# New orders for two convolutions and two attention layers, a softmax normalized on TensorE, and row statistics read from PSUM

## The chip, the cores and the metric

The kernel runs on one core of a Trainium2 chip. A core has several engines with instruction queues of their own: TensorE (PE in the profile, with its weight loads as PEld), VectorE (DVE), ScalarE (ACT), GpSimd (POOL) and SyncE (SP), which here only issues transfers. Each engine takes its instructions strictly in the order in which they were issued to it; an instruction that needs another engine's result waits at the head of its queue, and everything behind it waits too. SBUF is the working memory, PSUM the small memory into which TensorE writes its sums. The metric is the device time of one execution in microseconds (us).

## The reference, cut to what matters

The input u has 2048 tokens of 512 features. Two kinds of layers alternate, A, B, A, B, with the same weights in both rounds, and each adds its result to x:

```python
x = A_u
x = x + A(layernorm(x));  x = x + B(layernorm(x))
x = x + A(layernorm(x));  x = x + B(layernorm(x))

# A: a convolution along the tokens, done by FFT
P = exp(dt * A[:, :, None] * l);  K = einsum("dn,dnl,dn->dl", C, P, dt * B).real
y = irfft(rfft(u, 4096) * rfft(K, 4096))[:2048] + u * Dskip

# B: attention of 32 heads (16 features each) over 8 keys, 2 tokens apart, behind each token
q, k, v = split(x @ wqkv)
logits = einsum("bhsd,bhswd->bhsw", q, kg) * 16 ** -0.5      # kg, vg: k, v at s, s-2, ..., s-14
o = einsum("bhsw,bhswd->bhsd", softmax(logits), vg) @ wo
```

The spectrum of K depends on the weights alone, so it is computed once and used by both A layers.

## The kernel before, in words

The work falls into five stretches that follow one another.

**Spectrum of K.** `kgen` builds tables of powers, multiplies them, turns the sums into the spectrum, stores it in DRAM (`kt_scratch`), and normalizes x and does the first half of the forward transform of the first A layer beside it, into the tile `Z`. It runs by a written order: the string `KGEN`, whose words each name a step. Words that begin with `@` are steps of the first convolution.

**A convolution** (`a_steps`) goes over 16 groups of 32 features, numbered 0 to 15. A group passes through a pipeline of one-letter steps on four engines:

- `T`: TensorE transposes 8 blocks of `Z` into PSUM (tile `pt`, line 246);
- `t` or `a`: VectorE (`t`) or ScalarE (`a`) copies them to SBUF (`zt`, line 252);
- `X`: TensorE, second half of the transform (`xp`, line 258; its PSUM pool `psX` holds one tile, so `X` of a group waits until the tile of the group in front has been copied out);
- `c`: ScalarE copies `xp` to `xc` (line 264);
- `p`: VectorE multiplies by the spectrum `Kt` (`pab`, line 271); then `k` loads a later group's `Kt` on SP;
- `v`: TensorE, inverse transform (`vp`, line 287); `V`: ScalarE copies it to the tile `VT` (line 291). Group 15 is done in two halves; the second ones are `i` and `I`.

The first convolution's order is the end of `KGEN`; the second's is made from the same words. After the last `p`, VectorE computes four rows of one lane each for the lag 2048 (`kU`, lines 311 and 313), which only the last quarter of y needs.

**y and its norm.** `y_rows` (lines 323 to 327) makes two rows of tokens in one PSUM tile `ps_y` (pool `psS`, two tiles): two matmuls with `VT`, sometimes one for lag 2048, and one that adds x. A row needs all 512 features, so all 16 groups of `VT`; the first tile alone does columns 0 to 479 of its two rows first, which need groups 0 to 14 only. ScalarE copies the tile to x (line 1454); VectorE computes the rows' statistics from the copy (line 1117), and the rows are normalized (lines 1123 to 1133), transposed (1147) and copied (1150).

**Attention** (`b_layer`). TensorE projects q and k (1164) and v (1251); VectorE multiplies q by k shifted by each of the 8 offsets (`prodqk`, 1212 and 1214), TensorE sums over a head's features (`Lp`, 1236); the softmax follows; v, shifted by transfers (1275), is multiplied by the weights on VectorE (`prodpv`, 1346), summed by TensorE (`po`, 1356), copied by ScalarE (`oT`, 1367) and multiplied by wo (1385, plus x, 1390). Heads go in four groups i, tokens in two halves jh. The softmax of (i, jh): maximum over the keys (VectorE and TensorE, 1295 to 1303); for i = 2, 3 TensorE subtracts it with the matrices `ident` and `nident` in PSUM and ScalarE takes exp from there (1313 to 1316); TensorE sums over the keys (1321); ScalarE takes Ln and then Exp of the negative (1323, 1324); VectorE multiplies by that (1325). In the first B layer the rows of x are then normalized again and put through the first half of the next transform (`N`, lines 1430 and 1433).

**The order.** The instructions of y, its norm and the attention are planned in `b_layer` as small operations with names (`y0a`, `n0b`, `L103a`, `S20g`, `P38k`; the last letter counts the operations of a block). The long strings in `LAYERS` give the order in which they are issued, one string for each round; a `+` behind a name chooses VectorE (or the second of two engines) for an operation that can run on either. `Plan` estimates times only to decide how many dummy columns TensorE streams into a gap (line 1079); it moves nothing.

Of the kernel before, what the change touches and what calls it, by code (L numbers as in the profile page):

```python
# [11 lines left out]
ACT = mybir.ActivationFunctionType  # L12
# [95 lines left out]
def make_small_consts(nc, const):  # L108
# [11 lines left out]
    small = [("order", _bf(order), BF), ("ident", _bf(np.eye(128)), BF), ("nident", _bf(-np.eye(128)), BF),  # L120
# [10 lines left out]
    nc.gpsimd.memset(C["zero"][:], 0.0)  # L131
    C["eps"] = const.tile([128, 1], F32, name="eps")
# [76 lines left out]
def a_steps(nc, tc, C, Ng, kt_dram, load_w, layer, Z, es, es_y, psS=None):  # L209
# [44 lines left out]
    def second_stage(cg):  # L254
        xps[cg] = psX.tile([128, 2, 512], F32, name="xp", tag="psX")
# [4 lines left out]
    def second_stage_out(cg):  # L260
        xc, xp = fwork.tile([128, 8, 1, 128], BF, name="xc", tag="xc"), xps.pop(cg)
        xcs[cg] = xc
        for gs in parts(cg):
            nc.scalar.copy(xc[:, gs].rearrange("q g o l -> q (g o l)"), xp[:].rearrange("q h n -> q (h n)")[:, gs.start * 128:gs.stop * 128])  # L264

    def times_spectrum(cg):
        pab, xc, kt = pabp.tile([128, 8, 2, 128], BF, name="pab", tag="pab"), xcs.pop(cg), kts.pop(cg)
        pabs[cg] = pab
        for gs in parts(cg):
            n = gs.stop - gs.start  # L270
            a.last = nc.vector.tensor_tensor(pab[:, gs], xc[:, gs].to_broadcast([128, n, 2, 128]), kt[:, gs], ALU.mult)  # L271
        if layer and cg + KT_BUFS[layer] < 16:
            load_k(cg + KT_BUFS[layer])
        if cg == 14 and layer == 0:
            load_w()
# [13 lines left out]
    def inverse_out(cg, part=0):  # L289
        dst = VT[:].rearrange("k r j d -> k (r j) d")[:, :, cg * 32:(cg + 1) * 32].rearrange("k q (e g) -> k q e g", e=GE)  # L290
        nc.scalar.copy(dst[..., parts(cg)[part]], vps.pop((cg, part))[:].rearrange("k g (q e) -> k q e g", e=GE))  # L291

    a.step = dict(T=transposes, t=transposed, a=lambda cg: transposed(cg, True), X=second_stage, c=second_stage_out,
                  p=times_spectrum, v=inverse, V=inverse_out, i=lambda cg: inverse(cg, 1), I=lambda cg: inverse_out(cg, 1), k=load_k)
# [3 lines left out]
def a_layer(nc, tc, C, Xg, Ng, kt_dram, layer, Z, es_z, a=None):  # L298

    if a is None:  # L300
        with ExitStack() as es:
            es.enter_context(es_z)
            a = a_steps(nc, tc, C, Ng, kt_dram, None, layer, Z, es, ExitStack())
            with tc.manual_schedule():
                for word in KGEN.split():
                    if word[0] == "@" and word[1] != "k":
                        a.step[word[1]](int(word[2:]))
    VT, F1T, psS, tag, ident = a.VT, a.F1T, a.psS, "psg" if layer == 0 else "psS", C["ident"]
    kU = Ng[NG - 1]
    with tc.issue_after(a.last.ins):  # L310
        nc.vector.tensor_tensor(kU[0:1], Ng[0][0:1], C["klast"][:].unsqueeze(1).to_broadcast([1, 4, D]), ALU.mult)
# [1315 lines left out]
```

## Time and profile before

| | us |
|---|---|
| median of 3 runs (lowest, highest) | 425.97 (425.73, 428.2) |
| the profiled execution | 425.74 |
| its span, first to last instruction | 424.0 |
| VectorE busy | 398.6 |
| TensorE matmuls busy | 374.4 |
| ScalarE busy | 332.2 |

A profile shows one execution. "Busy" is the time in which an engine works on at least one instruction; two instructions of one engine may overlap a little, so the mean time of an instruction is longer than the distance from its start to the next one's start. In a row of a timeline the first number is the start, the second the time that the row covers, "x4" the instructions merged in it, and the bracket the idle time ahead of it with what ended it. The granted clock of TensorE is 1.00 throughout.

### The profile page before, as it was taken

The numbers are of one execution on the slowest core, as the hardware profiler recorded it, in microseconds if no ns is written. First come the engines' busy times: TensorE is split into PE (matmuls) and PEld (weight loads), VectorE is DVE, ScalarE is ACT, GpSimd is POOL, SyncE is SP. The second block draws the span as 40 slices with busy tenths as digits, with TensorE's granted clock in tenths as the row PEclk, the third lists the DMA queues.
The fourth block names the chain that finished last, engine by engine and source line by source line (L and its number), as shares of the span: only waits on it lengthen the run. The fifth ranks groups of instructions, "written<-read, shape, count | busy, mean of one in ns | idle before, by whom it ended". The sixth has DMA issues, their size and how long they took to land.

```text
span 424.0 us, 12183 instructions
## 1 busy us (share of the span) xinstructions
PE 374.4 (88%) x5072; PEld 258.1 (61%) x5112; DVE 398.6 (94%) x732; ACT 332.2 (78%) x602; POOL 25.5 (6%) x66
## 2 busy tenths in 40 slices
PE   1167998999989999999997899789999999996996
PEld 1033685676468755686865565278845686875563
DVE  5999999999889989899999999979989999999994
ACT  6999999998989989767655499989988676663542
POOL 5000011011210000002010000000000001200000
PEclk9999999999999999999999999999999999999999
DMA  7900002253889940005281061249300009350022
GB/s 227 430 32 0 2 17 52 74 162 109 254 242 280 300 146 3 2 2 119 58 175 52 2 198 54 100 117 284 101 0 4 2 2 162 69 123 2 22 80 101
DMA packets 25790, 44.06 MB, mean 104 GB/s; under 512 B 7301, under 2 KB 17222, under 8 KB 25094
## 3 DMA queue, kind: packets, MB, share of 16 engines
q1 hardware_dynamic: 22918, 38.09, 30.7%
q0 software_dynamic: 1856, 4.53, 4.8%
q8 instruction: 40, 0.66, 0.7%
q10 hardware_dynamic: 960, 0.66, 0.5%
q14 instruction: 16, 0.13, 0.1%
HBM read 29.01 MB, written 6.95 MB: 85 GB/s over the span
## 4 chain that ended last, share of the span: by engine, by line
PE 36%; DVE 28%; ACT 13%; issue 9%; DMA 3%; SPq 1%; DVEq 0%; ACTq 0%
DVE prodpv L1346 11%; PE ps_qk L1164 8%; DVE prodqk L1214 5%; PE ps_v L1251 4%; PE psg L578 3%; PE Lp L1236 3%; ACT Z L1433 2%; DVE Z L481 2%; PE psk L545 2%; DVE zt L252 2%; ACT xc L264 2%; DMA V<-V 2%; PE ps_y L327 2%; PE ps_y L323 2%; PE pt_x L1147 2%
## 5 line engine op out<-in xcount | busy, mean ns | idle before, releaser
L1346 DVE TENSOR_TENSOR prodpv<-V,Lsb 128x2048 bf16<-128x2048 bf16 x64 | 75.4, 1220 | 0.1
L1164 PE MATMUL ps_qk<-xnT,wqk 128*128 128x512 bf16 x256 | 60.1, 379 | 0.0
L1212 DVE TENSOR_TENSOR prodqk<-qT,N 128x1024 bf16<-128x1024 bf16 (+3 forms) x88 | 42.5, 541 | 2.1 <-ACT N L1167 1.8
L1214 DVE TENSOR_TENSOR prodqk<-qT,N 128x1024 bf16<-128x1024 bf16 (+3 forms) x56 | 40.6, 764 | 0.2 <-ACT qT L1167 0.2
L1356 PEld LDWEIGHTS <-prodpv 128*128 128x128 bf16 x1024 | 34.3, 98 | 9.6 <-DVE prodpv L1346 3.8
L271 DVE TENSOR_TENSOR pab<-xc,Kt 128x2048 bf16<-128x2048 bf16 (+1 forms) x34 | 39.1, 1159 | 0.9 <-ACT xc L264 0.6
L1356 PE MATMUL po<-halves,prodpv 128*128 128x64 bf16 x1024 | 37.3, 193 | 2.6 <-DVE prodpv L1346 2.6
L1164 PEld LDWEIGHTS <-wqk 128*128 128x128 bf16 x256 | 23.7, 98 | 23.5 <-DVE xnT L1150 0.2
L264 ACT CAST xc<-xp 128x1024 bf16<-128x1024 f32 (+1 forms) x34 | 35.7, 1066 | 1.4 <-PE pt L246 0.7
L291 ACT CAST VT<-vp 128x1024 bf16<-128x1024 f32 (+1 forms) x34 | 35.6, 1098 | 0.0
L287 PEld LDWEIGHTS <-pab 128*128 128x128 bf16 x512 | 30.9, 98 | 6.8
L287 PE MATMUL vp<-sb_IC,pab 128*128 128x128 bf16 x512 | 33.3, 219 | 0.6
L1385 PE MATMUL ps_o<-wo_t,oT 128*128 128x512 bf16 x122 | 31.9, 379 | 0.6
L1236 PEld LDWEIGHTS <-prodqk 128*128 128x128 bf16 x1024 | 29.4, 96 | 4.8 <-DVE prodqk L1214 1.9
L1367 ACT CAST oT<-po 128x512 bf16<-128x512 f32 x32 | 17.7, 587 | 18.4 <-PE po L1356 18.4
L1236 PE MATMUL Lp<-sb_bones,prodqk 128*128 128x8 bf16 x1024 | 30.3, 166 | 1.4 <-DVE prodqk L1214 1.2
L1251 PE MATMUL ps_v<-wv,xnT 128*128 128x256 bf16 x256 | 30.3, 272 | 0.0
L505 PE MATMUL psadd<-Z,sb_ident 128*128 128x512 bf16 (+3 forms) x72 | 18.7, 342 | 12.8 <-DVE Z L481 6.9
L1258 ACT CAST V<-ps_v 128x512 bf16<-128x512 f32 x32 | 18.6, 586 | 13.2 <-PE ps_v L1251 13.0
L1117 DVE BATCH_NORM_STATS2 ln_stats<-X 128x6 f32<-128x512 bf16 x39 | 24.9, 680 | 2.4 <-ACT X L1454 2.4
L1167 ACT CAST N<-ps_qk 128x512 bf16<-128x512 f32 x32 | 18.5, 590 | 10.4 <-PE ps_qk L1164 10.1
L1251 PEld LDWEIGHTS <-xnT 128*128 128x128 bf16 x256 | 24.3, 98 | 3.6
(195 smaller groups left out, 820.0 us busy)
## 6 DMA issues: line engine op xcount, KB each, us to landing
Kt<-kt_scratch SPq DMA_DIRECT2D x60, 256.0 KB
kt_scratch<-ks SPq DMA_DIRECT2D x32, 128.0 KB
G<-c_G SPq DMA_DIRECT2D x2, 1536.0 KB
V<-V SPq DMA_DIRECT2D x8, 288.0 KB
X<-in_A_u_dram SPq DMA_DIRECT2D x4, 512.0 KB
F1Tsb<-c_F1T SPq DMA_DIRECT2D x2, 1024.0 KB
V<-V SPq DMA_DIRECT2D x4, 512.0 KB
V<-V POOLq DMA_DIRECT2D x4, 384.0 KB, 8.4
```

The lines of the kernel that those rows point to most:

```text
L264: nc.scalar.copy(xc[:, gs].rearrange("q g o l -> q (g o l)"), xp[:].rearrange("q h n -> q (h n)")[:, gs.start * 128:gs.stop * 128])
L271: a.last = nc.vector.tensor_tensor(pab[:, gs], xc[:, gs].to_broadcast([128, n, 2, 128]), kt[:, gs], ALU.mult)
L287: a.last_pe = nc.tensor.matmul(vp[:, g, :], pabs[cg][:, gs.start + g, ab, :], C["IC"][:, ab, :], start=(ab == 0), stop=(ab == 1))
L291: nc.scalar.copy(dst[..., parts(cg)[part]], vps.pop((cg, part))[:].rearrange("k g (q e) -> k q e g", e=GE))
L1164: nc.tensor.matmul(t.ps[:], wqk[:, ct, f0:f0 + 128], x_group(g)[:, :, ct], start=(ct == 0), stop=(ct == 3))
L1212: nc.vector.tensor_tensor(b.pr[:, u:u + 2 * n, 1 - halves_of[0], :], q, cols(kT[i][:, starts[0]:starts[0] + n * 128]), ALU.mult)
L1214: nc.vector.tensor_tensor(b.pr[:, u:u + 2 * n].rearrange("f u a q -> f a u q")[:, ::-1], q.unsqueeze(1).to_broadcast([128, 2, 2 * n, 64]), ...
L1236: nc.tensor.matmul(t.Lp[:, w, u % 2, u // 2, :], b.pr[:, u].rearrange("f a q -> f (a q)"), bones[:], start=False, stop=(t.parts == W // 2 ...
L1251: nc.tensor.matmul(t.ps[:, jj, :], tokens(ct, jp * 2 + jj, c), wv[:, ct, fp * 256:(fp + 1) * 256], start=(jj + ct == 0), stop=(jj == 1 and ...
L1346: nc.vector.tensor_tensor(t.p2[:, c:c + k, 0:nj, :].rearrange("p c j (d h) -> p c j d h", d=DH), m.V2[i // 2][:, c0 + c:c0 + c + k, r0:r0 ...
L1356: nc.tensor.matmul(po[jj // k][:, jj % k, c, :], t.p2[:, c - c0, jj, :], fold, start=(first and c == c0 and jj % k == 0), stop=(last and c ...
L1385: nc.tensor.matmul(t["ps"][:], m.oT[:, ft, j * 128:(j + 1) * 128], wo_t[:, ft, :], start=(start and ft == lo), stop=(ft == 3 or kept and f ...
```

## The change

It has five parts.

1. **Orders of the convolutions.** The end of `KGEN` is rewritten, and the second convolution gets an order of its own, `CONV2`. Steps that go to another engine: in the first, the copy `t1` to VectorE (it was `a1`, ScalarE) and `W15`, the first half of the last copy to `VT`, to VectorE; in the second, `W9` and `J15` (copies to `VT` on VectorE). `c` and `p` of group 15 are cut into two words each. In the second the first three `xp` tiles come from the pool `psS` (`EARLY_X`).
2. **Lag 2048.** The four rows become words `U0`, `Y1`, `Y2`, `Y3` in the orders.
3. **y.** The first tile's cut is at column 448 instead of 480, the matmuls stand in another order, and for rows 0 to 3 (`raw`) the statistics are read from the PSUM tile `ps_y` instead of from the copy.
4. **Softmax.** In the first B layer, for i = 2 and 3 (`pe_den`): exp goes to a tile `e`, TensorE sums it, ScalarE takes Ln; then TensorE builds logits minus maximum minus 4 Ln(sum) anew (three matmuls, with a new matrix `nident4`), and ScalarE takes a second exp of that, which is the normalized weight. The Exp of line 1324 and VectorE's multiplication of line 1325 are gone there.
5. **Orders of both B layers**, anew, with the choices `+`. Both begin with the third tile of y (`y1a`: rows 4 and 5) and only then take the first (`y0a`). In the second layer the copies `oT` of i = 2, 3 may go to VectorE; one does (`P38k+`).

```diff
+    small = [("order", _bf(order), BF), ("ident", _bf(np.eye(128)), BF), ("nident", _bf(-np.eye(128)), BF), ("nident4", _bf(-np.eye(128) * DH ** 0.5), BF),
...
-        "@c15 @v14 @V13 @p15 @V14 @v15 @V15 @i15 @I15")
...
+        "s30 z15 f13 e33 f2 z13a z13v z2a z2v s31 o30 @T0 @k4 @T1 @t0 o31 e31 @t1 @X0 @c0 @T2 @t2 @T3 @p0 @k5 @X1 @T4 @c1 @X2 @a3 @c2 e30 "
...
+        "@T12 @t12 @U0 @X10 @v8 @V7 @c10 @T13 @X11 @V8 @p10 @k15 @t13 @c11 @p11 @v9 @T14 @X12 @V9 @c12 @v10 @V10 @t14 @p12 @T15 @X13 @v11 "
+        "@c13 @X14 @V11 @t15 @c14 @p13 @p14 @v12 @V12 @X15 @c15 @d15 @p15 @q15 @v13 @v14 @v15 @i15 @Y1 @Y2 @V13 @V14 @W15 @Y3 @I15")
+CONV2 = ("@T0 @T1 @t0 @a1 @X0 @T2 @X1 @c0 @U0 @c1 @t2 @p0 @p1 @T3 @T4 @X2 @a3 @v0 @X3 @c2 @c3 @T5 @v1 @t4 @V0 @p2 @t5 @X4 @c4 @T6 @V1 @v2 "
...
+        "@X13 @t14 @v11 @c13 @p12 @T15 @t15 @V11 @p13 @X14 @c14 @p14 @v12 @V12 @X15 @c15 @d15 @p15 @q15 @v13 @Y1 @v14 @v15 @i15 @Y2 @V13 "
+        "@V14 @V15 @J15 @Y3")
 PLUS = (13,)
...
+Y_CUTS = (0, 448, 512)
+EARLY_X = (0, 1, 2)
...
+    def y_rows(g, hf, row, ps, add):
+
+        if ps is None:
+            ps = psS.tile([128, 2, D], F32, name="ps_y", tag=tag)
+        steps = [(jj, slice(0, D)) for jj in range(2) if jj == row]
+        if g + hf == 0:
+            cuts = [slice(x, y) for x, y in zip(Y_CUTS, Y_CUTS[1:])]
+            steps = [(1, c) for c in cuts[1:]] if row else [(jj, cuts[0]) for jj in range(2)] + [(0, c) for c in cuts[1:]]
+        for jj, cols in steps:
+            j4 = hf * 2 + jj
+            j = g * 4 + j4
+            with tc.issue_after(a.last_pe.ins) if j + cols.start == 0 else nullcontext():
+                nc.tensor.matmul(ps[:, jj, cols], F1T[:, j, 0, :], VT[:, 0, j, cols], start=(cols.start == 0), stop=False)
+            if g == NG - 1:
+                nc.tensor.matmul(ps[:, jj, cols], C["last_tok"][:], kU[:, j4, cols], start=False, stop=False)
+            if add:
+                nc.tensor.matmul(ps[:, jj, cols], ident[:], Xg[g][:, j4, cols], start=False, stop=False)
+            nc.tensor.matmul(ps[:, jj, cols], F1T[:, j, 1, :], VT[:, 1, j, cols], start=False, stop=cols.stop == D)
...
-    dict(order="y0a y0b y0c y0d n0a n0b n0c n0e n0d n0h n0g n0i n0f y3a y3b n3a n3c y1a y1b n3b n1a n0j n0k y1c y1d n1b n0l n0p+ n0o+ n0m+ n0n "
...
+    dict(order="y1a y1b y0a y0b y0c n0a n0b n0c y0e y0f y0g n0e n0f n1a n1b n0i n0k n0h n0j n1c y0d n0d y1c y0h n0g y2a n2a y1d y3c n0l n0m y2b "
+               "y2c n1d n1e n0n n1f n1i n2c n0p+ n1g n0r n0o+ n1h n0q+ n2b t0a t0c y3d n1j n0s y3a n3a n1k n1l n1o+ n1n+ n1p+ t0b n1m t0d t1c "
...
-    dict(order="y0a y0b y0c y0d n0a n0c n0b n0d n0e n0g n0i n0h y1a y1b n1a n0f n1c n1b y1c y1d n1d n1e y2a n0j y2b y2c y3c n2a n0k n1i n0l n1g "
...
+    dict(order="y1a y1b y0a y0b y0c n0a n0b n0c y0e y0f y0g n0e n0f n0k n0i n1a n1b n0j n0h n1c y0d n0d y1c y0h n0g y2a y1d n0l y2b n2a y2c y3c "
+               "n0m n1e n1d n1i n0n n1h n1g n1f n0q+ n0o+ n0p+ n1j n1k t0a n1l n0r+ t0c y2d y3a n1p t0b y3d n0s n3a n1n+ n1m+ n1o+ n2c t0d t1a "
...
+               "P28k P28l P38b P38c P38e Raa Rda Rfa P38d P38j P38h Rbb Rdb Rab P38f Reb Rcb Rfb n2q n3q Xa P38l P38k+ Rec Rdc Red Rcc Rcd Rfc "
...
+         raw=[0, 1, 2, 3],
+         y_add=[],
+         pe_den=(2, 3),
+         ot_any=[],
...
+         pe_den=(),
+         ot_any=[2, 3],
...
-        plan = Plan({"-": 0.0, "PE": 0.0, "DVE": 0.5, "ACT": 0.5, "SP": 0.0, "POOL": 0.0, "dma": 0.0}, lay["keep"])
+        plan = Plan({"-": 0.0, "PE": 0.0, "DVE": 1.15, "ACT": 0.85, "SP": 0.0, "POOL": 0.0, "dma": 0.0}, lay["keep"])
...
+                if raw and 4 * g + jj in lay["raw"]:
+                    t, ps, rows = raw[jj // 2]
+                    o = plan.add("DVE", RAW_US, lambda jj=jj, t=t: nc.vector.bn_stats(st["stats"][:, jj, :], t["ps"][:, jj % 2, :]), [rows[jj % 2], first])
+                    stats.append((jj, o))
+                    if jj % 2:
+                        plan.add("-", 0.0, lambda: None, [d for _, d in stats[-2:]] + [got["y", g, jj // 2]], drop=ps[:1])
...
+            def less(k, u, by_den):
+                u.ps = psA.tile([128, W // 2, 128], F32, name="ps_sub", tag="psA")
+                nc.tensor.matmul(u.ps[:], ident[:], P()[:, k], start=True, stop=False)
+                nc.tensor.matmul(u.ps[:], C["nident"][:], t.mx[:, k].unsqueeze(1).to_broadcast([128, W // 2, 128]), start=False, stop=not by_den)
+                if by_den:
+                    nc.tensor.matmul(u.ps[:], C["nident4"][:], t.rdb[:, k].unsqueeze(1).to_broadcast([128, W // 2, 128]), start=False, stop=True)
+
+            def exp(k, u, out, bias):
...
+            if i in lay["pe_den"]:
+                o = plan.add("ACT", act_us(128 * n), lambda: nc.scalar.activation(t.rdb[:], t.den[:], ACT.Ln, scale=DEN_SCALE), [p], drop=[p])
+                for k in range(n):
+                    u = SimpleNamespace()
+                    p = plan.add("PE", 0.645, lambda k=k, u=u: less(k, u, True), [o], take=PA)
+                    got["P", i, jhs[k]] = plan.add("ACT", act_us(512), lambda k=k, u=u: exp(k, u, P, C["den_bias"][:]), [p], drop=[p] + [opened] * (k == n - 1))
+                return
...
-                def evict(n=n):
+                def evict(eng="ACT", n=n):
                     dst = m.oT[:, i, (j0 + n * k) * 128:(j0 + n * k + k) * 128].rearrange("f (j c q) -> f j c q", c=2, q=64)
-                    nc.scalar.copy(dst, po[n][:])
-                o = plan.add("ACT", act_us(512), evict, pes, drop=[takes[n]])
+                    (nc.scalar.copy if eng == "ACT" else nc.vector.tensor_copy)(dst, po[n][:])
+                us = dict(ACT=act_us(512), DVE=0.61)
+                o = plan.add(us if i in lay["ot_any"] else "ACT", us["ACT"], evict, pes, drop=[takes[n]])
                 for j in range(j0 + n * k, j0 + n * k + k):
```

144 lines of the change are left out of this document (83 added, 61 removed), and 127 rows, old and new, of tables (CONV2, KGEN, LAYERS, stores).

## The prediction

> **What bounds the kernel now.** First I read the head of the page and then the busy time by stage, cut where one stage's last wait ends: the first convolution, its y and norms, the middle of the first attention, its end with the next norms, and the same again for the second round up to the tail. Columns: TensorE, its weight loads, VectorE, ScalarE, GpSimd, then clock, DMA share, GB/s.
>
> ```profile
> span 424.0 us, 12183 instructions
> PE 374.4 (88%) x5072; PEld 258.1 (61%) x5112; DVE 398.6 (94%) x732; ACT 332.2 (78%) x602; POOL 25.5 (6%) x66
> ```
>
> ```profile
> 119.10:151.50 32.40, 29.76 (x410) 25.22 (x417) 30.68 (x35) 31.49 (x37) 1.12 (x8) 1.00 0.99 291
> 151.50:180.00 28.50, 28.36 (x207) 15.71 (x209) 25.65 (x70) 23.09 (x38) 0.00 (x0) 1.00 0.05 13
> 180.00:246.00 66.00, 61.47 (x1060) 46.19 (x1060) 65.96 (x115) 39.09 (x84) 4.46 (x8) 1.00 0.31 65
> 246.00:275.80 29.80, 27.25 (x312) 14.75 (x314) 29.04 (x59) 29.06 (x76) 0.00 (x0) 1.00 0.40 125
> 275.80:308.10 32.30, 29.70 (x409) 25.20 (x417) 29.00 (x32) 30.54 (x35) 0.00 (x0) 1.00 0.55 165
> 308.10:340.00 31.90, 31.77 (x276) 18.16 (x278) 29.23 (x79) 24.51 (x41) 0.00 (x0) 1.00 0.01 2
> 340.00:415.60 75.60, 70.96 (x1222) 52.96 (x1225) 75.12 (x120) 42.60 (x86) 4.46 (x8) 1.00 0.29 64
> 415.60:424.00 8.40, 4.52 (x33) 2.00 (x34) 2.77 (x5) 3.14 (x6) 0.00 (x0) 1.00 0.37 127
> ```
>
> Four things are to be seen. In the two long middles VectorE never rests (65.96 of 66.00, 75.12 of 75.60): only less work for it helps there. In the two heads TensorE is full (28.36 of 28.50, 31.77 of 31.90) and VectorE idles 2.85 and 2.67. In the two convolutions TensorE, VectorE and ScalarE are all within a tenth of full, so moving a copy between them gains little: TensorE's gaps, 2.64 and 2.60 us, are the most that an order can win. Between 246 and 275.8 VectorE and ScalarE are both full. The 425.74 us of the profiled execution are this span and 1.74 around it; the median, 425.97, lies 0.23 higher. I sum against 425.74.
>
> **The first convolution.** The rows around its end:
>
> ```profile
> 119.85 0.69 DVE L252 COPY zt<-pt 128x1024 bf16<-128x1024 bf16 x1 [0.79 <-PE pt L246]
> ...
> 122.32 1.23 DVE L271 TENSOR_TENSOR pab<-xc,Kt 128x2048 bf16<-128x2048 bf16 x1
> 123.46 0.68 DVE L252 COPY zt<-pt 128x1024 bf16<-128x1024 bf16 x1
> 124.06 1.22 DVE L271 TENSOR_TENSOR pab<-xc,Kt 128x2048 bf16<-128x2048 bf16 x1
> 129.45 1.23 DVE L271 TENSOR_TENSOR pab<-xc,Kt 128x2048 bf16<-128x2048 bf16 x1
> 131.29 1.23 DVE L271 TENSOR_TENSOR pab<-xc,Kt 128x2048 bf16<-128x2048 bf16 x1
> ...
> 150.40 1.21 DVE L311 TENSOR_TENSOR N<-N,klast 1x2048 bf16<-1x2048 bf16 x1
> 151.64 1.30 DVE L313 TENSOR_TENSOR N<-N 1x512 bf16<-1x512 bf16 x3
> 154.13 2.59 DVE L1117 BATCH_NORM_STATS2 ln_stats<-X 128x6 f32<-128x512 bf16 x4 [1.19 <-ACT X L1454]
> 149.39 3.07 ACT L291 CAST VT<-vp 128x1024 bf16<-128x1024 f32 x4
> 151.53 0.36 PE L323 MATMUL ps_y<-VT,F1Tsb 128*128 128x480 bf16 x1 [0.37 <-ACT VT L291]
> L1433 DVE CAST Z<-ps_s 128x512 bf16<-128x512 f32 x10 | 6.4, 678 | 0.0
> ```
>
> Before, the lag rows (1.21 and 1.30) run behind the last product, in time that VectorE spends waiting for y; and y begins at 151.53, when group 14 is in VT, though the last copy ends at 149.39 + 3.07 = 152.46. After, U0, Y1 and Y2 stand ahead of W15 on VectorE, t1 has come to it, and the first y tile is the one of rows 4 and 5, which needs all columns: y's first matmul waits for both halves of group 15. The cut at 448 no longer helps, as its tile comes second.
>
> VectorE's work from 119.85 on: its 30.68 us in the stage (U0's kind, 1.1 of it, is in there), plus t1 0.6, Y1 and Y2 0.8 (two of three of 1.30), W15 0.65 (a cast of 512 columns from PSUM has 0.68, less an overlap): 32.7, so W15 would end at 152.5. It can shrink: a product and a copy took 1.74 us from 122.32 to 124.06, when nothing waited, and 1.84 from 129.45 to 131.29, when all engines paced each other; over 16 groups that is up to 1.5, giving 151.0. I take 152.0, two thirds toward the row as it ran: y starts **0.5 late** (bounds -0.3 and +1.0). The Kt transfers do not let the stage end much sooner either, with a DMA share of 0.99.
>
> **The second convolution.** Its head loses time to the single xp tile:
>
> ```profile
> 278.87 0.59 PE L258 MATMUL xp<-zt,sb_C 128*128 128x512 bf16 x2 [0.21 <-ACT xc L264]
> 280.57 0.59 PE L258 MATMUL xp<-zt,sb_C 128*128 128x512 bf16 x2 [0.65 <-ACT xc L264]
> 308.13 0.36 PE L323 MATMUL ps_y<-VT,F1Tsb 128*128 128x480 bf16 x1 [0.37 <-ACT VT L291]
> 310.73 2.59 DVE L1117 BATCH_NORM_STATS2 ln_stats<-X 128x6 f32<-128x512 bf16 x4 [1.19 <-ACT X L1454]
> ```
>
> EARLY_X takes these two waits away (0.86), and W9 and J15 take 1.4 us of copies from ScalarE, which has 30.54 of 32.30. They cost VectorE 1.2 and 0.65: with Y1 and Y2 its 29.00 become 31.65, which from 276.44 (its first copy, 0.65 into the stage) would end at 308.1; shrunk by up to 1.5, 306.6. In the middle y starts at 307.4, **0.7 early** (bounds -1.4 and +0.3), all groups waited for.
>
> **y and the heads.** A tile of y, six matmuls, and what follows:
>
> ```profile
> 157.22 0.38 PE L323 MATMUL ps_y<-VT,F1Tsb 128*128 128x512 bf16 x1
> 158.51 0.38 PE L323 MATMUL ps_y<-VT,F1Tsb 128*128 128x512 bf16 x1
> 320.47 0.89 PE pt_x L1147 x16
> 321.37 6.04 PE ps_qk L1164 x28
> L1454 ACT CAST X<-ps_y 128x1024 bf16<-128x1024 f32 x16 | 16.1, 1008 | 4.0 <-PE ps_y L327 3.9
> L618 DVE CAST Z<-ps_s 128x512 bf16<-128x512 f32 x8 | 5.4, 690 | 2.9 <-ACT Z L620 2.7
> ```
>
> A tile takes 1.29. Reading statistics from PSUM saves the copy ahead of them, 1.0 of the 2.6 us from y's start to the first statistic (151.53 to 154.13); but the tile now stands behind one of 1.3. First statistic: start + 1.3 + 1.2 + 0.1 = 2.6 again. So the statistics move just as y does: 154.6 and 310.0. Its own duration I leave at the row's (2.59 for four); the nearest row from PSUM, 678 ns for 512 columns, of the first convolution's fence, says no more. [...]
>
> The statistics of rows 0 and 1 now stand ahead of ScalarE's copy of the same PSUM tile. The two casts of lines 618 and 620 also read one tile from two engines, and there VectorE waited 2.7 us for ScalarE, one after the other. So I let the copy wait for both statistics (1.2 us), which keeps the tile, one of two, and stops TensorE for about 0.7 at the fourth tile, in both rounds. [...]
>
> Against that, less stands ahead of the first attention product. In the first round 9 projections and 8 half-transpositions are ahead of it before, 6 and 4 after: 3 x 0.865 (6.04 / 7) + 4 x 0.445 = 4.4 us of TensorE; in the second 7 and 5 against 6 and 4, 1.3 us. Of VectorE's idle time beyond the first wait of 1.19, 1.66 and 1.48 us, I let the first order win half, **-0.8**, and the second, after the stall of 0.7, **-0.3** (bounds: nothing, and all).
>
> **Softmax, end and tail.**
>
> ```profile
> L1325 DVE TENSOR_TENSOR Lsb<-Lsb,sm_rdb 128x512 bf16<-128x512 bf16 x16 | 6.6, 420 | 0.0
> L1316 ACT ACTIVATE Lsb<-ps_sub 128x512 bf16<-128x512 f32 x8 | 4.8, 600 | 4.1 <-PE ps_sub L1314 4.1
> L1324 ACT ACTIVATE sm_rdb<-den 128x128 bf16<-128x128 f32 x16 | 4.4, 278 | 0.3
> L1131 ACT ACTIVATE N<-X,ln_nb,ln_rstd 128x512 bf16<-128x512 bf16 x4 | 3.3, 814 | 0.3 <-DVE ln_nb L1125 0.3
> 416.34 1.07 ACT L1367 CAST oT<-po 128x512 bf16<-128x512 f32 x2 [3.07 <-PE po L1356]
> 416.35 3.88 PE L1385 MATMUL ps_o<-wo_t,oT 128*128 128x512 bf16 x17
> ```
>
> Four multiplications of 0.42 leave VectorE, 0.34 each with the overlap of 0.08 that 122.32 + 1.23 against 123.46 shows: **-1.4** (bounds -1.7 and, if the longer way makes VectorE wait, +1.4). What is added, four times an exp of 0.60 for one of 0.28 on ScalarE and three matmuls of 0.216 on TensorE, lies where ScalarE idles 27 us of 66 and TensorE 4.5. The way to the weights grows by about 0.7 us; in the order three or four products or multiplications stand on VectorE meanwhile, about 2 us, which cover it. In the norms behind, two of sixteen rows go from VectorE to ScalarE and one of Z's copies the other way: nothing for VectorE, +0.9 for a ScalarE that is full; as half of it can start earlier, **+0.4** (0 to 0.9). At the tail one of the last two oT copies goes to an idle VectorE and lands 0.5 sooner, of which the 17 matmuls behind pass on **-0.2** (0 to -0.5).
>
> Sum: +0.5 - 0.8 - 1.4 + 0.4 - 0.7 - 0.3 - 0.2 = -2.5, so **423.2 us**.
>
> **Rivals.** *TensorE decides the heads, and gets later: slower, 428.3.* The place is the wait of y's first matmul for W15, behind a VectorE that the lag rows fill. If VectorE's work doesn't shrink, y starts 1.0 late in the first round and even in the second, the stall adds 0.7 twice, and as TensorE has 0.14 and 0.13 us free in the heads, neither the earlier products nor the shorter softmax are worth anything: +1.0 + 1.4 + 0.4 - 0.2 = +2.6. It decides once y starts more than about 1 us later than before. For it: both heads are full of TensorE. Against: TensorE's work can be postponed into the middles, where 4.5 us are free.
>
> *The orders win the idle time: faster, 419.7.* If both convolutions shrink to their bounds (-0.3, -1.4) and VectorE never idles in the heads (-1.66, -1.48) it is -4.8, and with softmax, end and tail at -1.2 it comes to -6.0. For it: the earlier first product. Against: TensorE's work ahead of everything else is unchanged.
>
> *The second exp comes late: 427.4.* Each of the four softmaxes makes VectorE wait 0.7: +2.8 in place of -1.4. For it: VectorE is full there, so every wait counts. Against: the products ahead of it.
>
> **Chances.** The forecast 0.55, TensorE late 0.17, idle time won 0.20, exp late 0.08. About 1% (4.3 us) is what a measurement of this kernel tells from no change. Faster by more than that is the second rival and an edge of the forecast, 0.24; slower by more only the far end of the first, with y's waits in both rounds above their bounds, 0.12; between 0.64. The range, 419.6 to 428.6, reaches to both outer rivals.
>
> **What will show it.** Right: y's first matmul near 152.0 and 307.4, released by a copy to VT from either engine; statistics near 154.6 and 310.0; the ScalarE copy of rows 0 and 1 starting only when VectorE is done with them; line 1325 gone from 16 to 12 with VectorE still full to the end of the middle. Wrong: VectorE idle ahead of `prodpv` in the first middle; more than 3 us of idle VectorE in a head; a convolution in which one engine falls clearly behind the others. The Kt transfers landing late, or a wait among the copies to VT, would spoil the first sum.

## The result, and the profile after

The changed kernel takes **428.98 us**, the median of 22 runs (426.91 to 430.63), against 426.81 for the kernel before (22 runs beside it, 425.56 and up): a ratio of 1.005, 95% interval 1.0035 to 1.0065. It is 2.2 us slower where I had forecast 2.5 us faster, and lies just above my range. One of before's 22 runs took 939.9 us, and one of the run with the old order of the moves of V, further on, took 631.98: the ratios leave both out, and without them the medians of these two are 426.69 in place of 426.81 and 428.06 in place of 428.50. The changed kernel's profiled run took 426.91 us, the lowest of the 22; that of before took 425.74, near its lowest. So the traces show 1.2 us of the loss, and another 1.0 is in ordinary runs and not in this trace. I come back to that.

The head of the page after, and its busy time in the same stages (TensorE, weight loads, VectorE, ScalarE, GpSimd, clock, DMA share, GB/s):

```profile
span 425.0 us, 12190 instructions
PE 376.5 (89%) x5076; PEld 258.5 (61%) x5119; DVE 398.8 (94%) x732; ACT 330.8 (78%) x598; POOL 26.0 (6%) x68
```

```profile
119.10:151.50 32.40, 29.77 (x409) 24.87 (x416) 31.49 (x39) 30.50 (x36) 1.12 (x8) 1.00 0.97 281
151.50:180.00 28.50, 26.62 (x175) 14.25 (x178) 22.87 (x64) 22.57 (x38) 0.00 (x0) 1.00 0.09 25
180.00:246.00 66.00, 64.47 (x1115) 48.48 (x1118) 65.73 (x114) 42.35 (x89) 4.46 (x8) 1.00 0.32 57
246.00:275.80 29.80, 27.42 (x285) 14.17 (x287) 29.57 (x58) 28.79 (x74) 0.00 (x0) 1.00 0.50 143
275.80:308.10 32.30, 29.47 (x409) 24.91 (x416) 30.99 (x38) 30.60 (x35) 0.00 (x0) 1.00 0.65 164
308.10:340.00 31.90, 30.45 (x270) 17.68 (x273) 26.96 (x74) 21.90 (x37) 0.00 (x0) 1.00 0.01 2
340.00:415.60 75.60, 72.42 (x1209) 53.91 (x1215) 75.16 (x123) 43.23 (x88) 4.41 (x8) 0.98 0.31 64
415.60:425.00 9.40, 5.52 (x54) 2.60 (x52) 4.90 (x7) 2.26 (x4) 0.00 (x0) 0.93 0.33 114
```

The middles look as before: VectorE is full (65.73 of 66.00, 75.16 of 75.60). The two heads do not. TensorE, which had 0.14 and 0.13 us to spare there, now has 1.88 and 1.45, and VectorE, which idled 2.85 and 2.67, idles 5.63 and 4.94: more than the 3 us that I had named as a sign of being wrong, in both heads. Both engines wait for each other. The timeline around y says where, in the first round and then in the second:

```profile
151.85 0.40 DVE L303 TENSOR_TENSOR N<-N 1x512 bf16<-1x512 bf16 x1
152.09 0.38 PE L339 MATMUL ps_y<-VT,F1Tsb 128*128 128x512 bf16 x1 [0.86 <-ACT VT L295]
...
154.89 2.59 DVE L1153 BATCH_NORM_STATS2 ln_stats<-ps_y 128x6 f32<-128x512 f32 x4 [2.64 <-PE ps_y L344]
...
156.27 1.01 ACT L1532 CAST X<-ps_y 128x1024 bf16<-128x1024 f32 x1 [1.68 <-DVE ln_stats L1153]
157.34 0.38 PE L339 MATMUL ps_y<-VT,F1Tsb 128*128 128x512 bf16 x1 [1.19 <-ACT X L1532]
...
159.87 0.70 DVE L1158 BATCH_NORM_STATS2 ln_stats<-X 128x6 f32<-128x512 bf16 x1 [0.95 <-ACT X L1532]
...
308.25 0.38 PE L339 MATMUL ps_y<-VT,F1Tsb 128*128 128x512 bf16 x1 [0.88 <-DVE VT L295]
...
311.05 2.59 DVE L1153 BATCH_NORM_STATS2 ln_stats<-ps_y 128x6 f32<-128x512 f32 x4 [2.63 <-PE ps_y L344]
...
313.50 0.38 PE L339 MATMUL ps_y<-VT,F1Tsb 128*128 128x512 bf16 x1 [1.19 <-ACT X L1532]
...
316.04 1.29 DVE L1158 BATCH_NORM_STATS2 ln_stats<-X 128x6 f32<-128x512 bf16 x2 [0.81 <-ACT X L1532]
```

Read it as a chain. VectorE's last lag row ends at 152.25, just behind y's start, and then it has nothing to do for 2.64 us until a tile with the right rows is there. Then it reads two rows, and ScalarE, idle for 1.68 us, copies that tile only behind these reads, at 156.27. The copy frees the tile, so TensorE stops for 1.19 us at its fourth tile, and the lateness of that tile comes back to VectorE as 0.95 us at a later statistic. The second round repeats it, with the same 1.19 and then 0.81.

The ledger of the two traces goes by five points on the path. Beside y's first matmuls (151.53 and 308.13 before, 152.09 and 308.25 after) these are TensorE's rows of before, then of after, in the timeline:

```profile
119.12 0.68 PE L246 MATMUL pt<-sb_ident,Z 128*128 128x128 bf16 x9 [0.23 <-DVE Z L618]
...
275.78 1.07 PE L246 MATMUL pt<-sb_ident,Z 128*128 128x128 bf16 x16 [0.92 <-ACT Z L1433]
...
415.66 0.64 PE L1356 MATMUL po<-halves,prodpv 128*128 128x64 bf16 x16 [0.26 <-DVE prodpv L1346]
```

```profile
119.12 0.68 PE L248 MATMUL pt<-sb_ident,Z 128*128 128x128 bf16 x9 [0.23 <-DVE Z L641]
...
276.18 1.00 PE L248 MATMUL pt<-sb_ident,Z 128*128 128x128 bf16 x15 [1.17 <-ACT Z L1489]
...
416.69 0.64 PE L1411 MATMUL po<-halves,prodpv 128*128 128x64 bf16 x16
```

| stretch | before | after | change | my sum |
|---|---|---|---|---|
| first transposition to y (first convolution) | 32.41 | 32.97 | +0.56 | +0.5 |
| y to the next transposition (first round) | 124.25 | 124.09 | -0.16 | -1.8 |
| to y (second convolution) | 32.35 | 32.07 | -0.28 | -0.7 |
| y to the last `po` (second round) | 107.53 | 108.44 | +0.91 | -0.3 |
| tail | 8.34 | 8.31 | -0.03 | -0.2 |

The first convolution is as forecast. The miss is in the two stretches that contain the heads.

### The profile page after: what moved, and what is told of

It reads as the page before. It is cut to its first block, busy times and chain, and to the rows that moved or that the text cites. A ratio compares the mean times of both kernels' runs of the same rounds, so it can differ in the third digit from the quotient of the medians.

```text
span 425.0 us, 12190 instructions
## 1 busy us (share of the span) xinstructions
PE 376.5 (89%) x5076; PEld 258.5 (61%) x5119; DVE 398.8 (94%) x732; ACT 330.8 (78%) x598; POOL 26.0 (6%) x68
## 5 line engine op out<-in xcount | busy, mean ns | idle before, releaser
L269 ACT CAST xc<-xp 128x1024 bf16<-128x1024 f32 (+1 forms) x34 | 34.7, 1035 | 2.2 <-PE xp L263 1.2
L295 ACT CAST VT<-vp 128x1024 bf16<-128x1024 f32 (+1 forms) x31 | 32.6, 1080 | 0.2 <-PE vp L291 0.2
L1208 ACT CAST qT<-ps_qk 128x512 bf16<-128x512 f32 x32 | 18.6, 585 | 11.5 <-PE ps_qk L1205 11.4
L1316 POOL DMA_DIRECT2D V<-V x16 | 8.9, 560 | 242.1 <-ACT V L1299 242.1
```

The source lines that it names most:

```text
L269: nc.scalar.copy(xcs[cg][:, gs].rearrange("q g o l -> q (g o l)"), xps[cg][:].rearrange("q h n -> q (h n)")[:, gs.start * 128:gs.stop * 128])
```

## The experiments

Each was timed beside the kernel before on the same chip, and its ratio is to that kernel. "Theory clock", the first one I tried, comes from the clock column: the changed kernel has 0.98 in its last middle where before had 1.00.

### The clock: fillers added, fillers removed

```profile
384.00:388.00 4.00, 2.88 (x50) 2.48 (x48) 4.00 (x8) 1.14 (x3) 0.00 (x0) 0.78 0.01 4
388.00:392.00 4.00, 3.26 (x44) 2.28 (x43) 4.00 (x4) 2.15 (x4) 0.00 (x0) 0.80 0.00 0
387.00:388.00 1.00, 1.00 (x24) 1.00 (x21) 1.00 (x4) 0.28 (x1) 0.00 (x0) 0.50 0.00 0
```

These are windows of the changed kernel, with the columns of the stages: TensorE pauses there (0.25 and 0.18 us busy in the two microseconds from 383 to 385), and the granted clock is 0.78 and 0.80, and 0.50 in the one microsecond of the last line. The planner asked for dummy columns just there, but ahead of softmax matmuls, whose functions don't stream any. The edit lets them:

```diff
                 t.ps = psA.tile([128, n, 128], F32, name="ps_max", tag="psA")
+                stream(t.ps[:], True)
                 nc.tensor.matmul(t.ps[:], swap, t.m2[:], start=True, stop=True)
...
                 u.ps = psA.tile([128, W // 2, 128], F32, name="ps_sub", tag="psA")
+                stream(u.ps[:], True)
...
                 t.den = psA.tile([128, n, 128], F32, name="den", tag="psA")
+                stream(t.den[:], True)
```

> The changed kernel, with the filler matmuls that its planner wants in the second round's middle (1,472, 128 and 384 columns, just ahead of the matmuls of one softmax) really issued; the planner asks for them there, but the softmax's functions don't issue any. Theory "clock": part of the loss is that TensorE, left idle between 382 and 385 us, is granted half the clock for some 4 us behind it; with the fillers the clock of that place stays at 1.00, the mean of the run goes from 0.99 to 0.995 or more, and the time falls from 428.98 by 0.7 to 2, to 427.0 to 428.3. Theory "y" (the loss sits in y's tiles and their statistics): nothing changes there, 428.7 to 429.3, whatever the clock does.

Measured 428.75 us, ratio 1.0048 (1.0032 to 1.0065). In the same place, which this run reaches 2.4 us later, the clock stays whole:

```profile
386.50:390.50 4.00, 3.11 (x75) 2.60 (x74) 4.00 (x8) 1.21 (x4) 0.00 (x0) 1.00 0.00 0
390.50:394.50 4.00, 3.26 (x59) 2.21 (x56) 4.00 (x4) 2.08 (x4) 0.00 (x0) 1.00 0.02 4
```

The opposite edit, to the kernel before:

```diff
-         keep=(0.85, 4600),
+         keep=(0.0, 0),
```

> The kernel before, without its filler matmuls (five were in its trace, at 231 to 240 and near 389 us). Theory "clock": without them the granted clock falls near 386 as in the changed kernel, the mean goes to 0.99, and the time rises by 0.7 to 2 us, to 427.5 to 429. Rival: the fillers, 1.4 us of matmuls in all, keep nothing: the clock stays at 1.00 and the time at that of before, 426.8 within 0.4.

Measured 425.96 us, ratio 0.9986 (0.9970 to 1.0002), with the clock down to 0.69:

```profile
384.00:388.00 4.00, 2.46 (x54) 1.88 (x52) 4.00 (x7) 1.14 (x3) 0.00 (x0) 1.00 0.00 0
388.00:392.00 4.00, 2.94 (x55) 2.68 (x52) 4.00 (x5) 1.56 (x3) 0.00 (x0) 0.69 0.00 0
```

So the clock came and went at that place as expected, and the time didn't follow: theory "clock" falls. VectorE is busy for the whole of all these windows, so it is likely that a slower TensorE only uses up its own slack.

### Where the statistics are read, and which rows come first

Four kernels make a square of two edits. Rows 0 and 1 first, with the statistics still from PSUM (the same in the second round's string):

```diff
-    dict(order="y1a y1b y0a y0b y0c n0a n0b n0c y0e y0f y0g n0e n0f n1a n1b n0i n0k n0h n0j n1c y0d n0d y1c y0h ...
+    dict(order="y0a y0b y0c n0a n0b n0c y1a y0d n0d y0e y0f y0g y1b n0e n0f n1a n1b n0i n0k n0h n0j n1c y1c y0h ...
```

> The changed kernel with y's tile of rows 0 and 1 ahead of the tile of rows 4 and 5 again, in both rounds; ScalarE's copy of rows 0 and 1 ahead of that of rows 4 and 5. All else stays, the statistics are still read from PSUM. Theory "y": y's first matmul waits for fewer columns (0.4 earlier, 151.7) and the first statistic comes 1.3 to 1.7 earlier (153.3); the copy still waits for both statistics, so TensorE still stops, now at the third tile. The heads lose 1.2 us less of VectorE each; with half of it kept to the end the time falls by 1.2 to 2.4, to 426.6 to 427.8. Theory "clock": no change, 428.7 to 429.3, as the place where the clock falls lies 75 us later. Rival: TensorE sets the heads, its stop only moves, and the time stays.

Measured 429.54 us, ratio 1.0058 (1.0035 to 1.0082): no gain, the outcome of the rival. The first statistic did come earlier, but now two pairs of statistics stand ahead of a copy, and TensorE stops twice. Its timeline in the first round, and then the windows of the two heads (30 us from y's first matmul on):

```profile
152.62 1.30 DVE L1153 BATCH_NORM_STATS2 ln_stats<-ps_y 128x6 f32<-128x512 f32 x2 [0.32 <-PE ps_y L344]
...
155.07 0.38 PE L339 MATMUL ps_y<-VT,F1Tsb 128*128 128x512 bf16 x1 [1.19 <-ACT X L1532]
...
156.56 1.29 DVE L1153 BATCH_NORM_STATS2 ln_stats<-ps_y 128x6 f32<-128x512 f32 x2 [2.64 <-PE ps_y L344]
...
159.01 0.38 PE L339 MATMUL ps_y<-VT,F1Tsb 128*128 128x512 bf16 x1 [1.19 <-ACT X L1532]
```

```profile
151.11:181.11 30.00, 27.51 (x183) 14.68 (x183) 24.16 (x67) 23.32 (x39) 0.00 (x0) 1.00 0.10 26
307.52:337.52 30.00, 27.52 (x186) 14.95 (x186) 24.72 (x68) 21.47 (x37) 0.00 (x0) 1.00 0.01 2
```

Statistics from the copied rows again, with rows 0 and 1 first (names of y's and the norm's operations as without `raw`):

```diff
-    dict(order="y1a y1b y0a y0b y0c n0a n0b n0c y0e y0f y0g n0e n0f n1a n1b ...
+    dict(order="y0a y0b y0c n0a n0b n0c y0d n0d n0e y1a y1b n1a n1b ...
-         raw=[0, 1, 2, 3],
+         raw=[],
```

> The changed kernel with y's first statistics read from the copied rows again, and y's tile of rows 0 and 1 first, as before; all later work stays in the changed order, the softmaxes and the convolutions too. Theory "held tile": in the two heads VectorE idled 2.85 and 2.66 us before (up to 30 us behind y's first matmul) and 5.64 and 4.95 in the changed kernel, since ScalarE's copy stands behind two statistics and the tile comes free 1.2 us late, and since the tile of rows 4 and 5 stands ahead. Without both, the heads idle about 3 us each again and the time falls from 428.98 by 3 to 5, to 424.0 to 426.0, below the kernel before. Rival "TensorE sets the heads": its stops go, but what stands behind y is as late, and the time falls by less than 1 us, 428.0 to 429.3.

Measured **422.82 us**, ratio 0.9915 (0.9886 to 0.9945): faster than both kernels, and 1.2 us below the range that I had expected. The same kernel was timed again later, on another chip:

> The kernel with statistics from the copied rows and rows 0 and 1 first once more, unchanged, beside the next one and beside the kernel before, as it was compared with others on another chip: 422.8, between 422.0 and 424.5, and faster than the kernel before by 2 to 4.

Measured 423.60 us, ratio 0.9921 (0.9901 to 0.9941). Its heads, cut likewise:

```profile
151.62:181.62 30.00, 30.00 (x243) 16.86 (x241) 26.72 (x72) 23.61 (x39) 0.00 (x0) 1.00 0.09 24
305.44:335.44 30.00, 30.00 (x272) 17.30 (x270) 27.15 (x74) 22.55 (x38) 0.00 (x0) 1.00 0.01 2
```

TensorE has no pause, and VectorE idles 3.28 and 2.85 us (5.84 and 5.28 in the kernel above). Its first wait for y is 1.36 us, though the lag rows have the same place in its convolution as in the changed kernel's. Its y begins with 14 groups, at 151.62, and VectorE works on until 152.81:

```profile
152.41 0.40 DVE L303 TENSOR_TENSOR N<-N 1x512 bf16<-1x512 bf16 x1
154.18 3.28 DVE L1108 BATCH_NORM_STATS2 ln_stats<-X 128x6 f32<-128x512 bf16 x5 [1.36 <-ACT X L1482]
```

Its second convolution, by the first transposition and y's first matmul in the timeline, takes 31.03 us:

```profile
274.41 1.05 PE L248 MATMUL pt<-sb_ident,Z 128*128 128x128 bf16 x16 [1.16 <-ACT Z L1439]
...
305.44 0.35 PE L339 MATMUL ps_y<-VT,F1Tsb 128*128 128x448 bf16 x1
```

The remaining corner, statistics from the copied rows but rows 4 and 5 first:

```diff
-    dict(order="y0a y0b y0c n0a n0b n0c y0d n0d n0e y1a y1b n1a n1b ...
+    dict(order="y1a y1b y0a y0b y0c n0a n0b n0c y0d n0d n0e n1a n1b ...
```

> As the run before it (statistics from the copied rows), but with the tile of rows 4 and 5 still first, as in the change: this sets the place of the tiles apart from where the statistics are read. Theory "held tile": TensorE's stops of 1.19 go, but VectorE's first wait grows from 2.64 to about 3.6 (two tiles of 1.3 and a copy of 1.0): 1 to 1.5 us slower than with rows 0 and 1 first, 425.0 to 427.5, and faster than the changed kernel. Rival: where the statistics are read makes no difference, 428.5 to 430.

Measured 428.50 us, ratio 1.0034 (1.0011 to 1.0057), slower than I expected, and at the edge of the rival's range: with rows 4 and 5 first, it makes little difference where the statistics are read. The first wait is the 3.6 us I had worked out, and the heads stay as idle as in the changed kernel, 5.53 and 4.85:

```profile
155.79 3.18 DVE L1108 BATCH_NORM_STATS2 ln_stats<-X 128x6 f32<-128x512 bf16 x5 [3.68 <-ACT X L1482]
```

```profile
151.95:181.95 30.00, 29.11 (x226) 16.12 (x228) 24.47 (x67) 22.96 (x37) 0.00 (x0) 1.00 0.07 19
307.94:337.94 30.00, 29.12 (x229) 16.35 (x232) 25.15 (x70) 21.63 (x36) 0.00 (x0) 1.00 0.01 2
```

| median us (ratio) | rows 4, 5 first | rows 0, 1 first |
|---|---|---|
| statistics from PSUM | 428.98 (1.005) | 429.54 (1.006) |
| statistics from the copy | 428.50 (1.003) | 422.82, 423.60 (0.992) |

Either edit alone costs the same 5 to 6 us as both, so undoing only one gains nothing. With either, VectorE idles 4.9 to 5.8 us in a head, and without both 2.9 to 3.3. Its waits for the tiles of y and their copies add up to this in the first round: 2.64 + 0.95 = 3.59 us with both edits, 3.68 with rows 4 and 5 first alone, 0.32 + 2.64 + 0.60 = 3.56 with the statistics from PSUM alone, 1.36 with neither. In the second they are 3.40 to 3.67 against 1.34. So the delays don't add up; once VectorE waits for the one, the other's falls into the same wait.

### The softmax on TensorE

```diff
-         pe_den=(2, 3),
+         pe_den=(),
```

> The changed kernel with the last two softmaxes of the first layer normalized by VectorE's multiplication again, in the same order of work. My prediction's step says that the change took 1.4 us from a VectorE that never rests there: undoing it costs 1.4, 430.4 (429.8 to 430.8). Rival "second exp late": the undone kernel is faster, 427.0 to 428.5. Theory "clock" says nothing on it unless TensorE falls idle in the first round's middle.

Measured 430.72 us, ratio 1.0102 (1.0077 to 1.0127): 1.7 us slower than the changed kernel by the medians, as the step said (1.4). In the traces of the changed kernel and of this one it is the row of VectorE's multiplication:

```profile
L1380 DVE TENSOR_TENSOR Lsb<-Lsb,sm_rdb 128x512 bf16<-128x512 bf16 x12 | 4.8, 414 | 0.1
```

```profile
L1380 DVE TENSOR_TENSOR Lsb<-Lsb,sm_rdb 128x512 bf16<-128x512 bf16 x16 | 6.4, 418 | 0.2 <-ACT sm_rdb L1379 0.2
```

### The convolutions' orders, and the second round

The changed kernel with the old orders of both convolutions (old words from the kernel before, `U0 Y1 Y2 Y3` behind the last product):

```diff
-         "... @V13 @V14 @W15 @Y3 @I15")
+         "... @p15 @q15 @U0 @Y1 @Y2 @Y3 @V14 @v15 @V15 @i15 @I15")
-EARLY_X = (0, 1, 2)
+EARLY_X = ()
```

> The changed kernel with both convolutions in their old orders (the lag rows behind the last product, all copies to VT on ScalarE, one xp tile). My prediction's steps: undoing the first convolution gives 0.5 back, undoing the second costs 0.7; by the traces 0.56 back and 0.28 lost. So 428.7 (428.2 to 429.5), y's first matmul 32.4 us behind the first transposition in both rounds. Rival: y, which in the changed kernel waits for all columns, waits 0.9 longer for a last copy on ScalarE, and it is 1 to 2 slower.

Measured 430.07 us, ratio 1.0071 (1.0044 to 1.0099): the new orders are worth 1.1 by the medians, the rival's size, though the two intervals overlap. The trace has the rival's wait too: its second convolution (280.31 to 313.62) takes 33.31 us, 0.96 more than before, and y's first matmul waits 1.35 for ScalarE's copy to VT. The same edit to the kernel with the copied rows and rows 0 and 1 first:

> The kernel with statistics from the copied rows and rows 0 and 1 first, with both convolutions in their old orders. The old orders in the changed kernel cost 1.1, where y waits for all columns in both; here y may begin at group 14 in both. By the traces the new orders bring the first matmul of y 0.5 earlier in the first round (31.94 against 32.41 us from the first transposition) and 1.3 in the second (31.02 against 32.35): 422.8 + 1.8 = 424.6 (423.8 to 425.4). Rival: the orders are worth nothing here, 422.5 to 423.2.

Measured 424.89 us, ratio 0.9963 (0.9946 to 0.9979): here they are worth 1.3 to 2.1, as expected, if runs on different chips may be compared; a run further on says otherwise.

The second round's attention as before:

```diff
-    dict(order="y1a y1b y0a y0b y0c n0a n0b n0c y0e y0f ...
+    dict(order="y0a y0b y0c y0d n0a n0c n0b n0d n0e n0g ...
-         raw=[0, 1, 2, 3],
+         raw=[],
-         ot_any=[2, 3],
+         ot_any=[],
```

> The changed kernel with the second round's attention as before: its order, statistics from the copied rows, both last copies to oT on ScalarE; convolutions and the first round as changed. Theory "held tile": the second head gives back 2.3 us of VectorE's idle time, the tail costs 0.2: 426.9 (426.2 to 427.8). Theory "clock" (fallen with the fillers, kept here as a check): the clock near 386 us returns to 1.00. Rival: the second round's order isn't what costs, 428.5 to 429.5.

Measured 427.13 us, ratio 1.0012 (0.9992 to 1.0033): 1.85 back, close to the 2.1 expected, so about that much of the loss is the second round's. It is not the head's alone: in the trace y comes 31.02 us behind the transposition (277.88 to 308.90) in place of 32.07, as it begins with 14 groups again, and only 0.85 is won behind y.

### What ordinary runs have beside the trace

Three traces showed VectorE waiting for Kt in the first convolution (1.7 us with the softmax undone, 1.5 with the old convolutions, 0.4 with the old second round). The edit, in the changed kernel and in the two with copied rows:

```diff
     def load_k(cg, eng=nc.sync):
+        if layer == 0 and cg >= 4:
+            kts[cg] = kts[cg - 4]
+            return
```

> The changed kernel, whose first convolution loads only the first four of its sixteen Kt tiles and multiplies with them again and again: this part of the computation is left out, and with it three quarters of the transfers of that stage. The traces of three runs (undone softmax, old convolutions, old second round) had a first convolution of 34.1 to 35.1 us in place of 33.0, with VectorE waiting 0.4 to 1.7 us for Kt. Theory "late Kt": that is what an ordinary run of the changed kernel has and its profiled one, the lowest of 22, had not; without the transfers the median falls by 1.5 to 2.5, to 426.5 to 427.5. Rival "no transfer": y's order costs what it costs without it, 428.4 to 429.3.

> The kernel with statistics from the copied rows and rows 0 and 1 first, with the same three quarters of the first convolution's Kt transfers left out. Its y begins with the columns of fourteen of the sixteen groups. Theory "late Kt": it can begin while the last two groups are late, so it loses less by them and gains less here: 0.3 to 1.0, to 421.8 to 422.5. Rival: nothing, 422.5 to 423.2.

> The kernel with statistics from the copied rows and rows 4 and 5 first, likewise without those transfers. The medians of the two orders lie 5.7 us apart, their profiled runs 2.0. Theory "late Kt": it falls by 2 to 3, to 425.5 to 426.5, and comes to some 3 to 4 us above the kernel with rows 0 and 1 first. Rival: the distance of 5.7 stays, 428.0 to 429.0.

Measured 429.86 (1.0064, 1.0041 to 1.0088), 425.05 (0.9958, 0.9939 to 0.9978) and 428.34 (1.0045, 1.0026 to 1.0064): none is faster beyond the scatter, and the second is even slower than with all transfers (on other chips), which stays unexplained. Beside it on its own chip the same kernel with the old orders of the convolutions, and all transfers, took 424.89, so there the new ones gained nothing, and their 1.3 to 2.1 is not settled. Late Kt is not the rest of the loss. But the trace of the first of the three has another wait, in its list of waits, and its stretch from 30 us behind y to the next transposition is long:

```profile
DVE prodpv L1404 <- DMA V<-V: 0.7, 1, 0.7
```

```profile
182.20:278.30 96.10, 91.53 (x1371) 61.82 (x1367) 93.61 (x167) 70.54 (x160) 4.46 (x8) 0.98 0.38 84
```

VectorE idles 2.49 us of it. The same stretch in the changed kernel's own trace, where that wait does not occur, has 0.65:

```profile
182.09:276.18 94.09, 89.80 (x1362) 60.93 (x1367) 93.44 (x167) 70.55 (x160) 4.46 (x8) 1.00 0.38 86
```

The kernel with copied rows and rows 0 and 1 first has two traces, the first with the wait (its window, and the row in the timeline) and the second without:

```profile
181.25:275.85 94.60, 89.55 (x1336) 60.90 (x1343) 92.31 (x164) 70.61 (x160) 4.47 (x8) 0.98 0.36 85
```

```profile
205.36 3.50 DVE L1351 TENSOR_TENSOR prodpv<-V,Lsb 128x2048 bf16<-128x2048 bf16 x3 [0.78 <-DMA V<-V]
```

```profile
181.62:274.41 92.79, 88.91 (x1344) 59.99 (x1342) 92.10 (x164) 70.63 (x160) 4.47 (x8) 1.00 0.37 87
```

94.60 against 92.79: one kernel, two runs, and the wait of 0.78 us for the moves of V goes with 1.8 us. In the order of the changed kernel the same holds: from y to the next transposition it is 124.09 us in its own trace, without the wait, and 126.09 and 126.10 in the two (fillers added, few Kt) where it is 0.7. The wait occurs in nine of the thirteen traces with the new order of the first round (the text below has eight of ten beside the changed kernel's own; it was nine of eleven), and in neither of the two with the old one. One thing that the new order changes there is the order of the nine moves, the largest now last on its queue. Put back:

```diff
-  ... V002b V013b M0m M0y M0g M0s M0a M0d M0j M0p M0v ...
+  ... V002b V013b M0a M0y M0m M0s M0g M0p M0j M0v M0d ...
```

> The changed kernel, with the nine moves of V within SBUF for the first pair of the first round issued in the old order, the largest (512 KB) first on its queue in place of last; nothing else is touched. In eight of the ten profiles that have the new first round's order behind y, beside the changed kernel's own, the first multiplication with V waited 0.3 to 1.0 us for these moves, and VectorE up to 1.1 us more for what followed; in the two of the old order it never did. Theory "late V": the order of the moves makes them land late in an ordinary run; the median falls by 0.7 to 1.8, to 427.2 to 428.3. Rival "V is as late": the moves take their 11 to 13 us in any order, and the shorter way of VectorE to its first multiplication is the cause: 428.6 to 429.3.

> The same kernel with the old order of the nine moves. Its profile showed the multiplication 0.8 us late for V, and 0.8 us of waits behind that. Theory "late V": 0.7 to 1.8 below the kernel beside it, 421.0 to 422.2. Rival "V is as late": the same as the kernel beside it within 0.4.

Measured 428.06 (1.0042, 1.0023 to 1.0061) and 423.42 (0.9924, 0.9897 to 0.9951; 423.60 beside it). By the ratios neither is faster beyond the scatter, and the second still waited 0.4 for V in its trace. In the first one's trace V was in time, and five of its runs lie at 427.07 to 427.77, where only two of the changed kernel's 22 lie below 428.3. So the order of the moves is not shown to be the cause, and for the changed kernel a part of it is not ruled out. What remains is likely that VectorE reaches its first multiplication by V so soon that the moves are just in time in some runs and late in others: the first of them is issued 41.5 to 41.6 us behind y's start in the traces of the changed kernel and of before, and the multiplication comes 54.69 us behind it in the changed kernel's, 56.19 in before's. That late V makes up the 1.0 us that the trace lacks is likely from its size, but not shown. There is a second candidate that no run tested: the first transposition, at 118.98 to 119.51 us in thirteen of the traces, comes at 120.72 to 121.05 in four. The runs leave it open.

## Why the prediction was wrong, step by step

**The heads failed.** The step read: "Of VectorE's idle time beyond the first wait of 1.19, 1.66 and 1.48 us, I let the first order win half, **-0.8**, and the second, after the stall of 0.7, **-0.3**". Three things in it were wrong.

- It kept the first wait at 1.19, since the first statistic stays 2.6 us behind y (measured 2.80). But before, VectorE did the lag rows in that time, for 1.41 us behind y's start, and after only for 0.16. I had named this cover myself in the first convolution, and did not count it where it was gone: the wait is 2.64, 1.45 more in each round. Moving the lag rows does not uncover the wait by itself. With copied rows and rows 0 and 1 first y begins ahead of VectorE's last copy to VT and lag row, which then fill 1.19 us, and the wait is 1.36 (1.34 in the second round). It is the tile that needs all columns, put first, that lets y begin only behind all of this work.
- The stop of TensorE was right in its cause and place (ScalarE's copy only behind both statistics, after a wait of 1.68 us; fourth tile), but it is 1.19 and not 0.7, and most of it comes back to VectorE as a wait, 0.95 and 0.81. The sum took it off in the second round alone, though the text has it in both. The two casts of lines 618 and 620, my nearest row, read different halves of their tile, so they bore on it less than I let them.
- Nothing was won. With both causes taken out, VectorE's idle time in the heads is 3.28 and 2.85 us, no less than the 2.85 and 2.67 of before: six projections ahead of the first product in place of nine (and of seven) won nothing.

In the place of -1.1 stand +2.78 and +2.27 of idle time. Part of it is work that VectorE now does ahead of y (30.68 and 29.00 us in the two convolutions before, 31.49 and 30.99 after); at the ends of the rounds it is +1.5 (-0.16 with the softmax's 1.7 taken out, where I had -0.8 and +0.4) and +0.9.

**The first convolution** was right in the trace (0.5; 0.56), y at 152.09 for 152.0. **The second** was too hopeful as long as y waits for all columns: 0.28 for 0.7. When y may begin with 14 groups, it is 31.03 us for 32.35, 1.3 early, about the bound that I gave to the rival "the orders win the idle time". I had seen that "the cut at 448 no longer helps" but not priced it: about 1 us in each round.

**The softmax** was right: -1.4, measured 1.7; in the changed kernel's trace no multiplication waited for the second exp, and that rival falls. **The statistic's own duration**: 2.59 for four from PSUM, as from the copied rows. **The tail**: -0.03 for -0.2.

**The rival "TensorE decides the heads"** gave 428.3 and came nearest, but for another reason. It needs y more than 1 us late and a full TensorE; y was 0.56 late in the first round and, counted from the transposition, 0.28 early in the second, and TensorE pauses in the heads (1.88 and 1.45 us). That its time came nearest was luck. My range ended just behind that rival, and no case in it had the lag rows' cover gone in both rounds.

Without the two edits to y the change gains 3.2 to 3.4 us on the kernel before. The softmax's 1.7 (measured in the changed kernel only) and the convolutions' 1.3 to 2.1 would make that up, with nothing from the heads; how it is shared between them is not shown.

## What to carry to other kernels

When work that used to fill a wait comes to stand ahead of it, because the work moves or because the wait begins later, reckon the wait again without it. Reading a PSUM tile from a second engine saved that reader the copy here (with rows 0 and 1 first, the first statistic comes 1.51 us behind y's start in place of 2.56) but held the tile until both had read it (ScalarE's copy waited 1.68 us for the statistics): with two tiles the producer stopped, for 1.19 us where the copy takes 1.01. When two edits feed the same wait, undoing either alone can gain nothing (here 429.54 and 428.50 us for 428.98, and 422.82 without both): undo them in pairs too.

## What the runs showed of the hardware that I had not expected

The granted clock fell to half in the changed kernel (0.50 from 387 to 388 us), and giving it back there with fillers saved no time that these runs can measure (428.75 us for 428.98). In the trace with the lowest span of all profiled runs (420.8 us, copied rows, rows 0 and 1 first) this window is part of the last middle:

```profile
380.00:384.00 4.00, 3.36 (x48) 2.80 (x47) 3.85 (x8) 1.65 (x5) 0.00 (x0) 0.50 0.00 0
```

In the changed kernel the fall followed a stretch in which TensorE did little: in windows of one microsecond it was busy for 0.25 and 0.18 us from 383 to 385, at a clock of 1.00, and from 386 to 390 the clock was 0.61, 0.50, 0.50 and 0.69. In the kernel before without its fillers, 2.46 us busy of 4.00 were followed by 0.69. With them it was busy for 0.22 us from 386 to 387 and 0.03 from 388 to 389, and the clock stayed at 1.00 up to 394, so what brings the fall is not shown. What the clock costs is another matter: where VectorE is full (4.00 us of 4.00), nothing was seen in the two filler runs (428.75 us for 428.98 with fillers added, 425.96 for 426.78 with them removed); in the window above, where VectorE is busy for 3.85 us of 4.00, no run tested it.

The moves of V within SBUF, issued at the same point of the order, were in time in one run and 0.78 us late in another of the same kernel. Over all traces with the new first round's order they were in time in five and 0.3 to 1.0 us late in ten.
